# Gated linear attention: a step of 128 tokens with its state brought to the middle, and TensorE in 64x64 tiles

## The chip, the core and the metric

The kernel runs on one core of one Trainium2 chip. The metric is the time of one execution on the device, in microseconds, as the median of several runs. TensorE (PE in the profile) does matrix products and transposes, VectorE (DVE), ScalarE (ACT) and GpSimd (POOL) work on 128 partitions, SyncE (SP) issues most transfers. TensorE writes into PSUM, which has eight banks of 128 x 512 fp32. Everything here is fp32, and an fp32 product is two MATMUL records in the profile, with a weight load (PEld) before each; a transpose is one.

## The reference, cut to what matters

There are 4 batches, 8 heads, 768 tokens and 48 channels a head.

```python
f = 1.0 / (1.0 + np.exp(-f_logit))
for t in range(S):
    state = f[:, :, t, :, None] * state + np.einsum('bhd,bhe->bhde', k[:, :, t], v[:, :, t])
    y[:, :, t] = np.einsum('bhd,bhde->bhe', q[:, :, t], state)
# x = y as (4*768, 8*48)
noisy_logits = x @ w_gate + np.log1p(np.exp(x @ w_noise)) * noise
# the two best of 8 experts, softmax over the two, then
# out[token] += weight * (relu(x[token] @ w1[e]) @ w2[e])
```

Per head and channel the state decays by f and gains an outer product of k and v; y reads it with q. The 3072 rows of y then go through a router to two of eight experts, each a pair of matrices 384x1024 and 1024x384.

## The kernel before

**Attention.** It is computed in 24 steps; step n is chunk c = n // 4 of 128 tokens (C) in batch b = n % 4. Heads stand in pairs: partitions 0 to 63 hold one head of a pair and 64 to 127 the other (`rows(par)`), four pairs side by side in the free dimension (`cols(hp)`). Within a step, with L the running sum of -log f, P = exp(-L) and Q = exp(L), the kernel forms qP = q·P and kQ = k·Q. The scores sc are kQ·qP for all 128x128 pairs of tokens of a head, masked to the causal ones (A, line 575). y is A·v (line 590) plus the part that comes from the state before the step, state·qP (line 601). The state after the step is (ds + state)·P at the step's last token, with ds = kn·v (line 596) and kn the transposed kQ (lines 566 and 568).

The work on one step is spread over several turns of the loop over i at the end, so that engines rarely wait for each other. In turn i the stages are, in this order: `forget` of step i+3 (transposes of f, exp, ln), `scaled` of i+1 (transposes of q and k, products with P and Q), `scores` of i, `summed` of i+2 (the running sum), `output` of i-1 (A·v, ds, the state's part, the new state), `decays` of i+2 (P and Q), `features` of i-2 (y times the router's weights and a reordering matrix, line 625, then the sums `lg` and the copy `xs` to memory). Between stages the loop takes one piece of the router of an earlier chunk (`route`), every third time one transfer of a list entry (`puts`), and near the end the first pieces of the experts. The order in which the program is written is the order on each engine; a helper, `in_order`, fixes it.

**What sets the order around the change.** Loads of f, q, k and v are issued on SP's queue inside these stages, each into a ring (5, 4, 4 and 6 buffers) and two to four steps ahead. PSUM: one pool of six single banks, given out in turn (`one_bank`), and one pair of banks for sc (`two_banks`). y takes two of the single banks. Products of K=64 and M=128 (sc), K=128 and M=64 (A·v, ds) and K=M=64 (the state's part) use half or a quarter of TensorE's array each.

**Experts.** From the end of attention to the end of the kernel two layers per expert run from gathered rows; none of this changes, except for which bank a product gets. Half of the tokens are routed before the second half of attention, so experts start as soon as attention ends. A check that no decay left the safe range (`beyond`, line 1181) stands behind the router.

Of the kernel before, what the change touches and what calls it, by code (L numbers as in the profile page):

```python
# [331 lines left out]
def kernel(  # L332
# [57 lines left out]
    XMIN, LMAX, LCAP = -40.0, 39.0, 60.0  # L390
    assert (H * D, H * DP, B * S) == (DM, 512, N)
# [15 lines left out]
    ps1 = ctx.enter_context(tc.tile_pool(name="ps1", bufs=6, space=PSUM))  # L407
# [3 lines left out]
    turns = [ps1]  # L411

    def one_bank(name):
        turns.append(turns.pop(0))
        return turns[-1].tile([128, 512], F32, tag="one", name=name)

    def two_banks(name):
        return ps2.tile([128, 2, 512], F32, tag="two", name=name)
# [26 lines left out]
    def counting(name, pattern, base=0, by_partition=0):  # L445
# [12 lines left out]
    causal = const.tile([128, 128], F32, tag="causal", name="causal")  # L458
    nc.gpsimd.affine_select(out=causal, in_=ones, compare_op=ALU.is_ge, fill=0.0, base=0,
                            pattern=[[1, 128]], channel_multiplier=-1)  # L460
    earlier = const.tile([128, 128], F32, tag="earlier", name="earlier")
# [47 lines left out]
    logf, L, P, Q, qP, kQ, A, kn, yT, lg = ({} for _ in range(10))  # L509

    def rows(par):
        return slice(par * DP, (par + 1) * DP)

    def cols(hp):
        return slice(hp * C, (hp + 1) * C)

# [11 lines left out]
    def transposed(nm, n):  # L528
        p = one_bank(f"{nm}p_{n}")
        flat = pads[nm][n % RING[nm]].rearrange("t h d -> t (h d)")  # L530
        for hp in range(HP):
            nc.tensor.transpose(p[:, cols(hp)], flat[:, cols(hp)], ident)  # L532
        return p
# [15 lines left out]
    def decays(n):  # L549
        P[n] = wk.tile([128, HP * C], F32, tag="P", name=f"P_{n}", bufs=4)  # L550
# [3 lines left out]
        nc.scalar.copy(far[:, n, :], L[n].rearrange("d (a t) -> d a t", t=C)[:, :, C - 1])  # L554

    def scaled(n):
        qP[n] = wk.tile([128, HP * C], F32, tag="qP", name=f"qP_{n}", bufs=3)
        nc.vector.tensor_tensor(qP[n], transposed("q", n), P[n], ALU.mult)
        kQ[n] = wk.tile([128, HP * C], F32, tag="kQ", name=f"kQ_{n}")
        nc.vector.tensor_tensor(kQ[n], transposed("k", n), Q[n], ALU.mult)  # L560

    def scores(n):
        if n // B < NCH - 1:
            kp = one_bank(f"kp_{n}")
            for hp in range(HP):
                nc.tensor.transpose(kp[:, cols(hp)], kQ[n][:, cols(hp)], ident)
            kn[n] = wk.tile([C, H, DP], F32, tag="kn", name=f"kn_{n}")
            nc.scalar.copy(kn[n].rearrange("t h d -> t (h d)"), kp)
        sc = two_banks(f"sc_{n}")
        for hp in range(HP):  # L570
            for par in range(2):
                nc.tensor.matmul(sc[:, par, cols(hp)], lhsT=kQ[n][rows(par), cols(hp)],  # L572
                                 rhs=qP[n][rows(par), cols(hp)], start=True, stop=True)
        A[n] = wk.tile([C, 2, HP * C], F32, tag="A", name=f"A_{n}")
        nc.vector.tensor_tensor(A[n].rearrange("j r (a i) -> j (r a) i", i=C), sc.rearrange("j r (a i) -> j (r a) i", i=C),  # L575
                                causal.unsqueeze(1).broadcast_to((C, H, C)), ALU.mult)

    def output(n):
        c, b = n // B, n % B
        vt = pads["v"][n % RING["v"]]  # L580


        y = [one_bank(f"y{odd}_{n}") for odd in range(2)]

        def at(hp, par):
            return y[hp % 2][rows(par ^ hp % 2), cols(hp // 2)]

        for hp in range(HP):
            for par in range(2):
                nc.tensor.matmul(at(hp, par), lhsT=vt[:, 2 * hp + par, :], rhs=A[n][:, par, cols(hp)],  # L590
                                 start=(hp < 2), stop=(c == 0 and hp >= HP - 2))
        if c < NCH - 1:
            ds = one_bank(f"ds_{n}")
            for hp in range(HP):
                for par in range(2):
                    nc.tensor.matmul(ds[rows(par), hp * DP:(hp + 1) * DP], lhsT=kn[n][:, 2 * hp + par, :],  # L596
                                     rhs=vt[:, 2 * hp + par, :], start=True, stop=True)
        if c:
            for hp in range(HP):
                for par in range(2):  # L600
                    nc.tensor.matmul(at(hp, par), lhsT=state[b][rows(par), hp, :],  # L601
                                     rhs=qP[n][rows(par), cols(hp)], start=False, stop=(hp >= HP - 2))
        yT[n] = wk.tile([128, 2, HP // 2 * C], F32, tag="yT", name=f"yT_{n}")
        for odd in range(2):
            nc.scalar.copy(yT[n][:, odd, :], y[odd][:, 0:HP // 2 * C])
        if c == NCH - 1:
            return

        dsv = wk.tile([128, HP, DP], F32, tag="ds", name=f"dss_{n}")
        nc.scalar.copy(dsv, ds[:, 0:HP * DP].rearrange("d (a e) -> d a e", e=DP))  # L610
        end = P[n].rearrange("d (a t) -> d a t", t=C)[:, :, C - 1:C].broadcast_to((128, HP, DP))
        new = wk.tile([128, HP, DP], F32, tag=f"st{b}", name=f"st_{n}")
# [757 lines left out]
```

## Time and profile before

| | |
|---|---|
| median of 14 runs | 664.78 us (661.1 to 673.97) |
| the profiled execution | 664.13 us, its span 662.1 us |
| TensorE busy | 642.7 us, 97% |
| VectorE, ScalarE, GpSimd busy | 442.5, 250.1, 264.3 us |
| attention | from the start to about 150 us; sc of step 0 starts at 13.6, of step 23 at 147.4 |
| queue q1 (transfers issued by SP) | 144,912 packets, 88.7 MB |

The profile is one execution. In rows of one stretch of time, busy time of every engine stands beside its number of instructions, then the clock granted to TensorE as a share of full speed, the mean busy share of the 16 DMA engines, and GB/s. In the chain of waits each line is a start, a length and what the end of the kernel waited for in that time.

### The profile page before, as it was taken

The numbers are of one execution on the slowest core, as the hardware profiler recorded it, in microseconds if no ns is written. First come the engines' busy times: TensorE is split into PE (matmuls) and PEld (weight loads), VectorE is DVE, ScalarE is ACT, GpSimd is POOL, SyncE is SP. The second block draws the span as 40 slices with busy tenths as digits, with TensorE's granted clock in tenths as the row PEclk, the third lists the DMA queues.
The fourth block names the chain that finished last, engine by engine and source line by source line (L and its number), as shares of the span: only waits on it lengthen the run. The fifth ranks groups of instructions, "written<-read, shape, count | busy, mean of one in ns | idle before, by whom it ended". The sixth has DMA issues, their size and how long they took to land.

```text
span 662.1 us, 13307 instructions
## 1 busy us (share of the span) xinstructions
PE 642.7 (97%) x5075; PEld 586.8 (89%) x5075; DVE 442.5 (67%) x1017; ACT 250.1 (38%) x611; POOL 264.3 (40%) x300
## 2 busy tenths in 40 slices
PE   8999999998999999999999999999999999999991
PEld 8999988886999899999999898998989989889891
DVE  7777867784647455445767767776776777766751
ACT  5876757652222212222332323333233233232320
POOL 7633886863267432123404224151341523513021
PEclk9999999999999999999999999999999999999996
DMA  9999989696589865652333495572954748701112
GB/s 185 200 210 213 197 192 193 139 341 183 162 249 259 215 210 179 185 143 49 60 108 76 122 309 162 189 214 82 314 169 121 230 132 294 190 3 25 21 25 29
DMA packets 157161, 108.90 MB, mean 164 GB/s; under 512 B 115536, under 2 KB 147280, under 8 KB 157088
## 3 DMA queue, kind: packets, MB, share of 16 engines
q1 hardware_dynamic: 144912, 88.70, 48.0%
q0 software_dynamic: 12176, 19.25, 13.6%
q8 instruction: 42, 0.69, 0.5%
q14 instruction: 31, 0.25, 0.1%
HBM read 88.56 MB, written 19.62 MB: 163 GB/s over the span
## 4 chain that ended last, share of the span: by engine, by line
PE 94%; DMA 2%; issue 1%; DVE 0%; POOL 0%; SPq 0%; POOLq 0%; DVEq 0%
PE y L986 32%; PE hp L878 13%; PE P L905 7%; PE W L905 4%; PE Z L905 4%; PE V L905 4%; PE X L905 4%; PE sc L572 4%; PE xp L625 4%; PE y L590 4%; PE xgp L827 2%; PE y L601 2%; PE fp L532 2%; PE kp L532 2%; PE ds L596 1%; PE qp L532 1%
## 5 line engine op out<-in xcount | busy, mean ns | idle before, releaser
L995 POOL DMA_INDIRECT out_dram<-ys,slots x48 | 81.7, 1701 | 211.3 <-ACT ys L1052 180.1
L986 PE MATMUL y<-qk_all,f_all 128*128 128x192 f32 x576 | 105.2, 326 | 0.0
L986 PEld LDWEIGHTS y<-qk_all,f_all 128*128 128x128 f32 x576 | 93.6, 190 | 0.2 <-DVE f_all L968 0.2
L878 PE MATMUL hp<-xt,w 128*128 128x256 f32 x384 | 87.2, 382 | 1.1 <-issue 1.0
L878 PEld LDWEIGHTS hp<-xt,w 128*128 128x128 f32 x384 | 71.7, 190 | 13.4 <-issue 3.9
L986 PE MATMUL y<-w,hs 128*128 128x192 f32 x384 | 70.8, 327 | 0.0
L986 PEld LDWEIGHTS y<-w,hs 128*128 128x128 f32 x384 | 63.7, 190 | 1.2
L968 DVE TENSOR_TENSOR f_all<-hs 128x512 f32<-128x512 f32 x48 | 32.4, 690 | 41.9 <-ACT hs L880 34.2
L810 POOL DMA_INDIRECT xg<-x_rows,slots x48 | 50.8, 1059 | 18.3 <-issue 10.7
L702 POOL DMA_INDIRECT lists<-entry,sloti x48 | 51.8, 1080 | 9.8 <-issue 9.3
L880 ACT ACTIVATE hs<-hp 128x512 f32<-128x512 f32 x32 | 19.1, 597 | 68.9 <-PE hp L878 62.4
L1052 ACT ACTIVATE ys<-ys,slots 128x384 f32<-128x384 f32 x24 | 14.8, 615 | 71.2 <-DVE ys L1051 69.4
L1126 POOL DMA_INDIRECT out_dram<-ys_q,slots_q x5 | 8.6, 1716 | 80.4 <-DVE ys_q L1124 80.4
L905 PE MATMUL P<-sides,v_all 128*128 128x256 f32 x128 | 38.1, 379 | 0.0
L575 DVE TENSOR_TENSOR A<-sc,causal 128x1024 f32<-128x1024 f32 x24 | 29.3, 1222 | 11.8 <-PE sc L572 9.1
L828 ACT COPY xt<-xgp 128x384 f32<-128x384 f32 x32 | 15.3, 478 | 56.7 <-PE xgp L827 56.7
L941 ACT ACTIVATE hs<-hs 128x256 f32<-128x256 f32 x32 | 13.4, 418 | 59.4 <-DVE hs L921 56.1
L1044 DVE TENSOR_TENSOR ys<-P,y 128x192 f32<-128x192 f32 x24 | 8.5, 354 | 39.9 <-PE y L986 25.1
L986 PE MATMUL y<-qk_all,hs 128*128 128x192 f32 x192 | 35.1, 326 | 0.0
L986 PE MATMUL y<-w,f_all 128*128 128x192 f32 x192 | 35.1, 326 | 0.0
L905 PE MATMUL X<-xt,w 128*128 128x256 f32 x128 | 32.8, 379 | 0.0
L905 PE MATMUL Z<-xt,v_all 128*128 128x256 f32 x128 | 32.8, 379 | 0.0
(189 smaller groups left out, 1381.9 us busy)
## 6 DMA issues: line engine op xcount, KB each, us to landing
w<-in_moe_w_dram SPq DMA_DIRECT2D x28, 1536.0 KB
w_q<-in_moe_w_dram SPq DMA_DIRECT2D x10, 1536.0 KB
f_all<-in_f_logit_dram SPq DMA_DIRECT2D x24, 192.0 KB
qk_all<-in_q_dram SPq DMA_DIRECT2D x24, 192.0 KB
qk_all<-in_k_dram SPq DMA_DIRECT2D x24, 192.0 KB
v_all<-in_v_dram SPq DMA_DIRECT2D x24, 192.0 KB
x_rows<-xs SPq DMA_DIRECT2D x24, 192.0 KB
out_dram<-zero SPq DMA_DIRECT2D x24, 192.0 KB
```

What stands on the lines that cost most here:

```text
L532: nc.tensor.transpose(p[:, cols(hp)], flat[:, cols(hp)], ident)
L572: nc.tensor.matmul(sc[:, par, cols(hp)], lhsT=kQ[n][rows(par), cols(hp)], rhs=qP[n][rows(par), cols(hp)], start=True, stop=True)
L575: nc.vector.tensor_tensor(A[n].rearrange("j r (a i) -> j (r a) i", i=C), sc.rearrange("j r (a i) -> j (r a) i", i=C), causal.unsqueeze(1). ...
L590: nc.tensor.matmul(at(hp, par), lhsT=vt[:, 2 * hp + par, :], rhs=A[n][:, par, cols(hp)], start=(hp < 2), stop=(c == 0 and hp >= HP - 2))
L625: nc.tensor.matmul(xp[:, hp, :], lhsT=yT[n][:, hp % 2, cols(hp // 2)], rhs=w_rt[:, hp, :], start=True, stop=True)
L702: into = nc.gpsimd.indirect_dma_start(out=lists, out_offset=bass.IndirectOffsetOnAxis(ap=sloti[:, r, b:b + 1], axis=0), in_=entry[:, c, b, ...
L810: nc.gpsimd.indirect_dma_start(out=xg[p][:, s, :], out_offset=None, in_=x_rows[0:HALF * B * C] if p < E else x_rows, in_offset=bass.Indire ...
L878: nc.tensor.matmul(hp[:, o, :], lhsT=w1[home(k)][:, i, (fo + o) * 128:(fo + o + 1) * 128], rhs=xt[k][:, i, :], start=(i == 0), stop=(i == ...
L905: nc.tensor.matmul(to, lhsT=x, rhs=y, start=start, stop=stop)
L968: nc.vector.tensor_tensor(sm[which], x, y, op)
L986: nc.tensor.matmul(P[name], lhsT=x[:, o, :], rhs=y[:, o, :], start=(o == 0), stop=(o == FH - 1))
L995: into = nc.gpsimd.indirect_dma_start(out=out, out_offset=bass.IndirectOffsetOnAxis(ap=slots[p][:, s, 2:3], axis=0), in_=ys[s], in_offset= ...
```

## The change

Tokens attend to each other only within 64 of a step's 128. A state in the middle of the step, `half` = ds of the first 64 tokens + the state before, carries the rest to the second 64. So sc and A·v have two 64x64 blocks on the diagonal for each head in place of one 128x128, and ds is made apart for the two halves. The matmuls are all 64x64 tiles at 64 columns, ordered so that four that follow one another use four different quarters of the array.

- `output` is split: `advance` (ds, `half`, the new state) now belongs to the same turn as `scores`, `output` (A·v and half of the state's part) to the next, `finish` (the other half and the copy to SBUF) to the turn after that.
- `upright` (transposing kQ) is a stage of its own, a turn before, and runs in the last chunk too. `scaled` runs a turn earlier. The order of the stages in a turn is new, and loads follow it.
- PSUM: four single banks with fixed users (bank 0: q and kn, 1: k and the first ds, 2: the second ds, `features`, 3: f and the router), a pair for sc and a pair for y, each with one buffer.
- The new state is made from `half`, the second ds and P's last column, kept in `far`, which held L's.
- The clears of the output and the empty lists are issued some steps later.

```diff
-    ps1 = ctx.enter_context(tc.tile_pool(name="ps1", bufs=6, space=PSUM))
+    ps1 = ctx.enter_context(tc.tile_pool(name="ps1", bufs=1, space=PSUM))
...
+    turns = [(ps1, n) for n in (0, 1, 3)]
+
+    def one_bank(name, which=None):
+        if which is None or which != 2 and done["turned"]:
+            turns.append(turns.pop(0))
+            pool, which = turns[-1]
+        else:
+            pool = ps1
+        return pool.tile([128, 512], F32, tag=f"bank{which}", name=name)
...
     def scores(n):
-        if n // B < NCH - 1:
-            kp = one_bank(f"kp_{n}")
-            for hp in range(HP):
-                nc.tensor.transpose(kp[:, cols(hp)], kQ[n][:, cols(hp)], ident)
-            kn[n] = wk.tile([C, H, DP], F32, tag="kn", name=f"kn_{n}")
-            nc.scalar.copy(kn[n].rearrange("t h d -> t (h d)"), kp)
         sc = two_banks(f"sc_{n}")
         for hp in range(HP):
-            for par in range(2):
-                nc.tensor.matmul(sc[:, par, cols(hp)], lhsT=kQ[n][rows(par), cols(hp)],
-                                 rhs=qP[n][rows(par), cols(hp)], start=True, stop=True)
+            for par, k in ((0, 0), (1, 1), (0, 1), (1, 0)):
+                nc.tensor.matmul(sc[rows(k), par, hp * T:(hp + 1) * T], lhsT=kQ[n][rows(par), part(hp, k)],
+                                 rhs=qP[n][rows(par), part(hp, k)], start=True, stop=True)
...
+    def from_state(n, phase):
+        was, y = held[n]
+        for hp in range(0, HP, 2):
+            for par, odd in ((0, 0), (1, 0), (0, 1), (1, 1)):
+                k = par ^ phase
+                if was[k] is not None:
+                    nc.tensor.matmul(y[rows(par ^ odd), k, (hp + odd) * T:(hp + odd + 1) * T], lhsT=was[k][rows(par), hp + odd, :],
+                                     rhs=qP[n][rows(par), part(hp + odd, k)], start=False, stop=(phase == 1 and hp == HP - 2))
+
+    def finish(n):
...
+        from_state(n, 1)
+        yT[n] = wk.tile([128, HP, 2, T], F32, tag="yT", name=f"yT_{n}")
+        nc.scalar.copy(yT[n].rearrange("e a r t -> e r a t"), held[n][1][:, :, 0:HP * T].rearrange("e r (a t) -> e r a t", t=T))
+
+    def advance(n):
...
+        for hp in range(HP):
+            for k, par in ((0, 0), (1, 1), (0, 1), (1, 0)):
+                if k < len(ds):
+                    nc.tensor.matmul(ds[k][rows(par), hp * DP:(hp + 1) * DP], lhsT=kn[n][rows(k), 2 * hp + par, :],
+                                     rhs=vt[rows(k), 2 * hp + par, :], start=True, stop=True)
...
+        if c:
+            nc.vector.tensor_tensor(half, dsv[0], state[b], ALU.add)
+        else:
+            nc.vector.tensor_copy(half, dsv[0])
+        before[n] = state[b], half
+        if last:
+            return
+        dss = wk.tile([128, HP, DP], F32, tag="ds", name=f"dss_{n}", bufs=1)
+        nc.scalar.copy(dss, dsv[1])
...
+        nc.gpsimd.tensor_tensor(mid, dss, half, ALU.add)
+        nc.gpsimd.tensor_tensor(new, mid, far[:, n, :].unsqueeze(2).broadcast_to((128, HP, DP)), ALU.mult)
...
     def output(n):
...
+        y = two_banks(f"y_{n}", "y")
         for hp in range(HP):
+            for k, par in ((0, 0), (1, 1), (0, 1), (1, 0)):
+                nc.tensor.matmul(y[rows(par ^ hp % 2), k, hp * T:(hp + 1) * T], lhsT=vt[rows(k), 2 * hp + par, :],
+                                 rhs=A[n][rows(k), par, hp * T:(hp + 1) * T], start=(hp == 0),
+                                 stop=(c == 0 and k == 0 and hp == HP - 1))
+        held[n] = before[n], y
+        from_state(n, 0)
...
-    for nm, n in (("f", 0), ("f", 1), ("q", 0), ("k", 0), ("f", 2), ("f", 3), ("q", 1), ("k", 1), ("v", 0)):
+    for nm, n in (("f", 0), ("f", 1), ("q", 0), ("k", 0), ("f", 2), ("q", 1), ("k", 1), ("f", 3), ("v", 0), ("q", 2), ("k", 2)):
         load(nm, n)
...
-        for stage, lag in ((forget, -3), (scaled, -1), (scores, 0), (summed, -2), (output, 1), (decays, -2), (features, 2)):
+        for stage, lag in ((upright, -1), (summed, -2), (finish, 2), (decays, -2), (scores, 0), (advance, 0), (output, 1), (scaled, -2), (forget, -3), (features, 2)):
```

## The prediction

> **What bounds the kernel now.** I read the page's busy times first, then the stretches of the span with every engine beside the others, then the chain of waits for one step of the attention part, then ScalarE's order of time in the same step.
>
> ```profile
> span 662.1 us, 13307 instructions
> PE 642.7 (97%) x5075; PEld 586.8 (89%) x5075; DVE 442.5 (67%) x1017; ACT 250.1 (38%) x611; POOL 264.3 (40%) x300
> ```
>
> TensorE is busy for 97% of the span, so a step gets shorter only if TensorE's own list gets shorter. The shares of the other engines are averages over attention and experts; the stretch 60 to 80 us is attention alone. Its columns are the length, then busy time and instructions of TensorE, its weight loads, VectorE, ScalarE and GpSimd, then granted clock, DMA share and GB/s:
>
> ```profile
> 60.00:80.00 20.00, 20.00 (x285) 18.42 (x284) 15.76 (x46) 14.47 (x40) 13.85 (x18) 1.00 0.94 198
> ```
>
> Here VectorE stands at 79%, ScalarE at 72%, GpSimd at 69% and the DMA at 0.94. TensorE is the bound with little room behind it: a change that takes a fifth of TensorE's work brings the others to their limits. The chain of waits (start, length, what) shows one whole step between two starts of sc, 6.00 us apart:
>
> ```profile
> 32.48 1.09 PE sc L572 x16
> ...
> 66.53 0.44 PE fp L532 x4
> ...
> 67.41 0.44 PE kp L532 x4
> ...
> 68.28 1.09 PE sc L572 x16
> 69.37 1.02 PE y L590 x16
> 70.40 0.46 PE ds L596 x16
> 70.86 0.60 PE y L601 x16
> 71.46 1.08 PE xp L625 x8
> ...
> 147.36 1.09 PE sc L572 x16
> ...
> 152.86 0.97 issue
> ```
>
> Four sets of transposes at 0.44 and these five make 6.01 us, and no wait stands between them. Each matmul has two records. ScalarE in that step:
>
> ```profile
> 67.43 0.50 ACT L630 COPY xs<-xp 128x384 f32<-128x384 f32 x1
> 67.80 0.63 ACT L537 ACTIVATE f<-fp 128x512 f32<-128x512 f32 x1
> 68.46 0.63 ACT L538 ACTIVATE f<-f 128x512 f32<-128x512 f32 x1
> 69.12 0.20 ACT L541 COPY cap<-f 128x4 f32<-128x4 f32 x1
> ...
> 69.88 0.57 ACT L568 COPY kn<-kp 128x512 f32<-128x512 f32 x1
> ```
>
> The reader is to see the spacing from one start to the next: 0.37 after xs, 0.66, 0.66, 0.11 after cap.
>
> **TensorE's list.** Two spacings carry the sum. Four transposes of 128 columns take 0.44, so 0.110 each; ds, eight pairs of 64 columns, takes 0.46, so 0.058 a pair. With 0.110 for each of eight pairs sc would take 0.88, y 0.88, xp 0.88, and the state's four groups of four 0.44: what is over, 0.21, 0.14, 0.20 and 0.16, I call the entry that each change of tile shape costs. The changed step has 64x64 tiles in sc, A·v and ds: eight groups of four at 64 columns. A group of four is not in the trace at 64 columns, only at 128, in the state's rows. One cut of that stretch, for these rows alone (columns: length, TensorE busy and records, weight loads, clock, DMA):
>
> ```profile
> 76.78:76.82 0.04, 0.03 (x4) 0.03 (x4) 1.00 1.09 219
> ```
>
> Four matmuls start within 0.04 us, and the next four only 0.11 after them: four tiles do run beside each other. So a group of four at 64 columns lies between 0.058 (columns decide, as in ds) and 0.115 (two pairs, one after the other). I take 0.058, since the state's four cost no more than one transpose of as many columns. Then sc, A·v and ds cost 0.46 each, the state's two halves 0.23 each (half of them a step later, in `finish`), transposes 1.76, xp 0.88, and two entries instead of four, 0.40: 4.88 against 6.01, so 1.13 less in each of the 16 steps of chunks 1 to 4. Chunk 0 has no state's part before (5.41 a step), and after it half of the tiles but as many groups: 0.53 less. Chunk 5 has no kp and no ds before (5.11); the change keeps both there, with ds in half the tiles and as many groups: 0.23 less. Sum 16x1.13 + 4x0.53 + 4x0.23 = 21.1 us off TensorE.
>
> **What becomes late instead.** First y: the accumulator is now one tile of two banks with a single buffer, so A·v of step i-1 waits until ScalarE has copied the y of step i-2 that `finish` completed in the same step. ScalarE's order puts ahead of that copy: exp, ln and cap of f, xs, kn. From the end of fp: hand-over 0.19, 0.66, 0.66, 0.11, 0.37, kn about 0.5, the copy of 128x512 about 0.58 (kn's row; the two halves of before take 0.65), hand-over 0.1: 3.17. TensorE's list from fp's end to A·v is xp 0.88, kp 0.44, entry 0.20, finish 0.23, sc 0.46, ds 0.46: 2.67. TensorE waits 0.50. Behind it in its queue stand A·v, the half of the state's part and the next three sets of transposes; VectorE's qP and kQ wait for those. It holds in the 17 steps that still have an f to transpose: +8.5 us. Its bounds are 0 (copies ahead of it move) and 0.9 (xs late).
>
> Second the start. The stretches from 10 to 40 us move 196 to 206 GB/s at a share of 0.95 to 1.03, so a load of 196.6 KB lands each 0.98 us. The first lands at 0.81+2.65=3.46. v of step 1 is load 19 now (18 before), so it lands near 21.1. Before, y of step 1 stood behind the second step's sc at 22.8 and never felt it. Now ds belongs to step 1 itself. From 21.1: ds, A·v, half state, entry, three transposes, kp, entry, finish make 3.5, so sc of step 2 is near 24.6, of step 3 near 29.9 and of step 4 near 35.4, where it stood at 32.48: +3.0 us (bounds +1.5 and +4).
>
> Third the small ones. VectorE: A drops from 1.22 to qP's 0.69 (same shape), the new half costs between the 0.35 of a 192-column and the 0.69 of a 512-column add, I take 0.42: about 0.1 less of 4.7 a step, hidden while TensorE has 4.88. But lg now often stands behind a piece of the router (max and index, about 0.36) and xs behind it: +0.1 in 17 steps, 1.7 us (bounds 0 and 0.36 each). GpSimd: chunk 0 gains a mid of 0.75 in each of four steps and the start two small copies for the mask, chunk 5 nothing: nothing waits for the new state until four steps later. SP's queue: q and k are asked for in the same step but behind v; `finish` adds no DMA; the clears of out and the empty lists move a few steps later, behind loads that run three steps ahead. Four single-column matmuls near the end: under 0.3 each, 1 us at most, in the range.
>
> Sum against the profiled execution's 664.1: -21.1 +8.5 +3.0 +1.7 = -7.9, so 656.2. The median of the 14 runs, 664.78, stands 0.65 above it: 657.
>
> **A rule against it.** The state's rows show four starts within 0.04 us. The Trainium skill, page "TensorE: Matmul & The Clock Gate", section "Wait — 56ns, not 53.3ns?", says that starts of matmuls never come closer than about 25 ns however few columns they have. By that, 128 records of a step's tiled part would take 3.2 us in place of 1.86, the sum would end near 681, and the change would be slower. The row shows some 10 ns between starts on different tiles, so I do not use it.
>
> **Rivals.** (1) TensorE alone sets the step: ScalarE is early enough and y never waits. For it: ScalarE has 28% idle. Against: the order above. -21.1+3.0 gives 646.7. (2) The DMA sets it. 0.94 of 6.0 us is 5.64 us of transfers a step, clears included; if that is need and not queueing, 17 steps shrink by 0.37 only, with the start +3.0 : 661.5. For it: share 0.94 to 1.03. Against: loads run far ahead of use (q of step 9 is issued at 39.75 and transposed near 60.6). (3) The other side: TensorE runs out of instructions. A step has 90 matmul records before and 152 after, each with its weight load; the page's instruction queue moved 0.69 MB for TensorE's 10,150, so 12 KB a step become 21, through the same crowded engines. The 0.97 us "issue" at 152.86, which no semaphore explains, is what such a gap would look like (my reading, not shown). One such gap in each of 20 steps is +19.4, so 676.6; it decides from 0.4 us a step on. Against: at 6.0 us a step it is rare. (4) The change does not do what it says: groups of four come as two pairs, 0.115. 32 groups of 0.057 more in 24 steps is +44, less the 8.5 of waits that this hides: 692. It decides from 0.08 a group.
>
> **Numbers.** Main 0.52, (1) 0.14, (2) 0.16, (3) 0.13, (4) 0.05. Within 0.5% (3.3 us, about what this measurement can tell from no change) lie half of (2), a little of the main case and of (3). Faster 0.70, same 0.10, slower 0.20. The main case's own range, from the bounds of its three waits, is 650 to 663; with (1) and the near half of (3) 645 to 670.
>
> **What would show it.** sc and A·v at 0.46 to 0.55 for 32 records; ScalarE's yT ending just before A·v starts; a TensorE wait of half a microsecond in each step at A·v; sc of step 4 near 35 us and the last sc near 139. Wrong if ds or sc take 0.9, if unexplained gaps spread over the steps, or if waits stand at kQ or at loads.

## The result, and the profile after

The changed kernel takes 692.03 us (median of 10 runs, 689.51 to 695.16) against 665.16 us (median of 47 runs of the kernel before): a ratio of 1.040, 95% interval 1.037 to 1.043. The forecast was 657.0, range 645 to 670. It was wrong by 35 us and on the wrong side.

First the page of the changed kernel: its span, TensorE's busy time and count, and the span in 40 slices (TensorE's busy tenths, then the clock granted to it, 17.3 us a slice).

```profile
span 690.9 us, 16424 instructions
...
PE 641.2 (93%) x6635; PEld 584.2 (85%) x6635; DVE 437.9 (63%) x1041; ACT 251.0 (36%) x591; POOL 263.6 (38%) x306
...
PE   7899887775999999999999999999999999999992
...
PEclk9999999996999999999999999999999999999997
```

TensorE has 1560 more pairs of weight load and matmul than before and is busy for 641.2 us, 1.5 less than before, in a span that is 28.8 longer. The start is idle as before; the fifth to the tenth slice, 69 to 173 us, are new. The stretches say more. Columns: length, busy time and instructions of TensorE, its weight loads, VectorE, ScalarE and GpSimd, then granted clock, DMA share, GB/s.

```profile
28.00:60.00 32.00, 29.66 (x822) 27.25 (x818) 22.76 (x53) 24.85 (x63) 14.86 (x18) 1.00 0.90 191
...
80.00:100.00 20.00, 16.89 (x445) 14.91 (x445) 13.16 (x28) 12.16 (x30) 16.32 (x23) 1.00 0.87 178
...
140.00:160.00 20.00, 12.78 (x298) 11.28 (x288) 10.86 (x29) 8.76 (x21) 12.82 (x17) 0.93 1.02 340
160.00:180.00 20.00, 14.17 (x233) 12.54 (x235) 7.92 (x21) 4.46 (x12) 3.60 (x8) 0.73 0.46 118
```

From 28 to 60 us TensorE works about as forecast. From 80 to 180 us it is busy for 13 to 17 of 20 us, and no other engine takes over: VectorE falls to 8 to 13 us, ScalarE to 4 to 12. The clock is lower as well, 0.93 from 140 to 160 us and 0.73 from 160 to 180. The trace's clock rows have 20.5 us at half speed between 100 and 175 us; the kernel before has none between 9 and 650 us.

The chain of waits in a step at 35 us is the forecast's own picture (start, length, what):

```profile
35.15 0.61 ACT f L549
...
35.78 0.64 ACT f L550
...
36.44 0.20 ACT cap L553
36.64 0.38 ACT xs L661
37.02 0.49 ACT kn L579
37.50 0.50 ACT yT L609
...
38.04 0.69 PE y L646 x32
```

fp is ready, ScalarE works through exp, ln, cap, xs, kn and yT with nothing between, and A·v starts 0.04 after yT's end. A·v of neighbouring steps starts at 32.72, 38.04, 43.36 and 48.69: 5.32 apart, where the forecast's main case had 5.38. The 32 matmuls of A·v start within 0.48 us, in eight groups of four tiles, 0.058 us from group to group.

The chain in a late step is a different kernel:

```profile
153.35 0.33 PE sc L585 x18
153.69 1.03 issue
154.72 0.28 PE sc L585 x2
155.00 1.14 issue
156.14 0.29 PE sc L585 x2
...
163.53 1.14 issue
164.67 0.26 PE ds L619
```

TensorE issues one to three matmuls and then nothing for about a microsecond, over and over for twelve microseconds, and no semaphore is named. Counted from the records, weight loads included, 42 start between 153.4 and 166.0 us; each of the steps between 36 and 53 us has 272 to 310 in 5.3 to 5.4 us. Up to 175 us there are 36 such gaps of over 0.4 us from record to record without a semaphore, 23.8 us in sum; the kernel before has 8, 5.2 us in sum. Within a train the gaps follow each other every 0.70 us or twice that. What runs beside them is on GpSimd (start, length, engine, line, operation, out<-in):

```profile
155.55 0.99 POOL L733 DMA_INDIRECT lists<-entry,sloti  x1 [0.21 <-issue]
...
156.84 0.97 POOL L733 DMA_INDIRECT lists<-entry,sloti  x1 [0.23 <-issue]
...
158.11 0.97 POOL L733 DMA_INDIRECT lists<-entry,sloti  x1 [0.23 <-issue]
```

These are the indirect DMAs that write list entries (`puts`, line 733), one every 1.28 us. 34 of the 35 gaps after 65 us lie beside an indirect DMA or within a microsecond of one; so do all 8 of the kernel before, the longest of them here:

```profile
153.18 0.97 POOL L702 DMA_INDIRECT lists<-entry,sloti  x1 [0.23 <-issue]
153.83 0.27 PE L601 MATMUL y<-qP,st 64*64 64x128 f32 x1 [0.97 <-issue]
```

In both kernels 0.7 of the time from 65 to 175 us lies so near to an indirect DMA. For the 8 the match is therefore weak, for the 34 of 35 it is a pointer; the experiments decide. TensorE's waits up to 200 us (waiting line, what it waited for, sum in us, times, longest) put the rest beside them:

```profile
PE sc L585 <- issue: 8.3, 14, 1.1
PE ds L619 <- issue: 5.9, 9, 1.1
PE kp L577 <- DVE kQ L572: 4.0, 6, 1.8
PE fp L544 <- DVE at L724: 3.6, 3, 1.2
PE y L646 <- ACT yT L609: 2.0, 7, 0.3
PE kp L577 <- DVE lack L757: 1.9, 1, 1.9
```

Two of the named waits are not in the forecast: fp waits for `at` and kp for `lack`, two small readings of the router by VectorE. (Of the wait at kQ, 3.3 of the 4.0 us stand in the first 25 us.) The router's products now share bank 3 with f's transposes, or take one of the three banks that rotate, and VectorE does them behind qP and kQ.

### The profile page after: what moved, and what is told of

Its sections match the earlier page's. It is cut to its first block, busy times and chain, and to the rows that moved or that the text cites. A ratio compares the mean times of both kernels' runs of the same rounds, so it can differ in the third digit from the quotient of the medians.

```text
span 690.9 us, 16424 instructions
## 1 busy us (share of the span) xinstructions
PE 641.2 (93%) x6635; PEld 584.2 (85%) x6635; DVE 437.9 (63%) x1041; ACT 251.0 (36%) x591; POOL 263.6 (38%) x306
## 4 chain that ended last, share of the span: by engine, by line
PE 84%; issue 4%; ACT 3%; DVE 3%; DMA 2%; SPq 1%; POOL 0%; POOLq 0%; DVEq 0%; ACTq 0%
PE y L1017 31%; PE hp L909 12%; PE P L936 6%; PE Z L936 4%; PE V L936 4%; PE X L936 4%; PE W L936 4%; PE xgp L858 2%; PE y L646 2%; PE y L600 2%; PE xp L656 2%; PE sc L585 2%; PE qp L544 2%; PE ds L619 2%; DMA v_all<-in_v_dram 1%
## 5 line engine op out<-in xcount | busy, mean ns | idle before, releaser
L1026 POOL DMA_INDIRECT out_dram<-ys,slots x48 | 80.1, 1669 | 231.1 <-ACT ys L1083 195.1
L558 DVE TENSOR_TENSOR_SCAN L<-f,cap 128x512 f32<-128x512 f32 x24 | 29.9, 1244 | 9.1 <-ACT cap L553 8.2
```

The lines of the kernel that those rows point to most:

```text
L558: nc.vector.tensor_tensor_scan(L[n], data0=logf[n], data1=cap[n % 2].rearrange("d a t -> d (a t)"), initial=0.0, op0=ALU.add, op1=ALU.min)
L1026: into = nc.gpsimd.indirect_dma_start(out=out, out_offset=bass.IndirectOffsetOnAxis(ap=slots[p][:, s, 2:3], axis=0), in_=ys[s], in_offset= ...
```

## The experiments

Three theories. **B**: indirect DMAs that GpSimd issues one behind the other slow the arrival of TensorE's instructions, and the changed kernel is more sensitive. **A**, the nearest to rival (3): TensorE's instructions are fetched too late because it executes more of them. **C**: the loss is waits for VectorE, ScalarE and loads. Ratios are to the kernel before on the same chip and in the same group of runs; steps are counted by the first record of their sc. Up to e14 a step of the changed kernel is that of the profile above. When e15 ran the kernel once more, its steps 5 to 8 took 16.6 us where that profile has 17.4, so less than a microsecond between two runs says nothing.

### Without the writes, more writes, later writes

**e1.** The writes are left out.

```diff
-            into = nc.gpsimd.indirect_dma_start(
-                out=lists, out_offset=bass.IndirectOffsetOnAxis(ap=sloti[:, r, b:b + 1], axis=0),
-                in_=entry[:, c, b, r, :], in_offset=None)
```

> The changed kernel without its 48 indirect writes of list entries (the puts on GpSimd); the lists stay empty, so the gathers read row 0, the experts work on the wrong rows and nothing is added to the output: the output is not the reference's. Theory B (indirect DMAs that GpSimd issues one behind the other slow the arrival of TensorE's instructions): the 35 TensorE gaps over 0.4 us without a semaphore before 175 us (23.8 us) go down to at most 8 gaps (5 us), which lie beside the gathers of 144 to 154 us; the first hp, at 177.2 us, moves to 152 to 158; time 664 to 673. Theory A (TensorE's instruction blocks are fetched too late because it executes more instructions per microsecond): gaps and time as they are, 687 to 693. Theory C (the loss is waits for VectorE, ScalarE or loads): 687 to 693.

675.33 against 665.46 (1 run): ratio 1.015. 10 gaps with 7.4 us are left; eight of them lie at 134 to 142 us beside the six indirect reads (line 841 of the changed kernel). The first hp starts at 160.1. Each of the three lies a little beyond what theory B gave (at most 8 gaps and 5 us, 152 to 158, 664 to 673). A and C, which expected no gain, are out as main causes; but 10 us of loss are left.

**e2 and e3.** Eight further writes, into arrays that nobody reads, in steps that have none; the second in the kernel before.

```diff
+            if spares and i >= 5:
+                nc.gpsimd.indirect_dma_start(out=spares.pop(0), out_offset=bass.IndirectOffsetOnAxis(ap=line, axis=0),
+                                             in_=empty[:, 0, :], in_offset=None)
+                nc.gpsimd.memset(spacer, 0.0)
```

> The changed kernel with eight further indirect writes (128 rows of 16 bytes, each into a spare array of its own) issued by GpSimd one behind the other in the two steps from the fifth on, about 40 to 51 us, where the changed kernel has no indirect DMA and one unexplained TensorE gap. Theory B: gaps of 0.5 to 0.7 us without a semaphore appear in that stretch, 2 to 6 us in sum (0.6 us a microsecond of burst would be 6, its later steps give less beside single writes), and the time grows by as much. Theory A: none appear, since the instructions of TensorE are the same; time within 1 us. Theory C: within 1 us.

> The kernel before with the same eight further indirect writes in its fifth and sixth step. Theory B with a price per instruction: the steps of before hold 90 matmuls in 6 us against 152 in 5.3, so the gaps come to less, 0 to 2.5 us (its own bursts between 95 and 158 us have 4.5 us of gaps in 22 us). Theory B with a price per write whatever runs: as much as in the changed kernel, 2 to 6 us. Theory A: nothing.

Changed kernel: 699.74 (1.051). From step 5 to step 8 it takes 24.60 us against 17.40 without them: 7.2 us, 0.9 a write; there are 8 gaps there, 5.0 us in sum. Kernel before: 673.98 (1.013); from step 5 to 8 it takes 21.89 against 17.99: 3.9 us, 0.5 a write, with 5 gaps, 2.8 us. That is more than a price per instruction allowed (0 to 2.5) and less than the same price per write. The chain of e2 at the place of the second group of three:

```profile
50.44 0.15 PE ds L623 x2
50.58 0.42 issue
51.00 0.31 PE ds L623 x3
51.31 0.41 issue
51.72 0.63 PE ds L623 x26
```

The trains of gaps can be made at will, by adding to GpSimd's list, with TensorE's own list unchanged. This shows that the indirect DMAs hold up TensorE; that it is the arrival of its instructions that they slow, as B puts it, is not shown. A second thing is shown, by one run each: the same eight writes cost the changed kernel nearly twice as much as the one before.

**e4.** The writes of chunks 3 and 4 wait until attention is over.

```diff
-            if puts and (slot % 3 == 0 or n_routed >= HALF):
+            if puts and (slot % 3 == 0 or n_routed >= HALF) and len(n_put) < HALF * B * 2:
```

> The changed kernel with the indirect writes of chunks 3 and 4 held back until attention is over (the writes of chunks 0 to 2 stay, since the first gathers need them). Theory B: the twelve microseconds of gaps between 153 and 166 us go, and with them the low clock after it; the writes then lie beside the experts, where bursts of eight have no gap at 215 to 226 us; the gaps at 77 to 136 us stay: time 674 to 682, ratio to the kernel before 1.015 to 1.025. Theory A: 687 to 693, since the same instructions run at the same rate. Theory C: 687 to 693.

684.44, ratio 1.029 (1.022 to 1.037): the direction of B, 7.6 us less, but short of 674 to 682. The train at 153 to 166 us is gone. In its place the experts have 3.6 us of gaps beside the writes that are now there, in one row of 15 indirect DMAs from 195 to 216 us and another of 17 up to 246. In the changed kernel itself the rows beside the experts, eight at the most up to 240 us, had none.

**e11.** The same edit in the kernel before.

> The kernel before with the indirect writes of chunks 3 and 4 held back until attention is over, as in the run that did so in the changed kernel. If a burst beside the attention steps is what costs: the burst of eight at 147 to 157 us and its 2.6 us of gaps go, and the writes lie beside the experts: 1 to 4 us less, ratio 0.994 to 0.999. If the first experts' matmuls, which run from 148 us on in the kernel before, are slowed as much wherever the burst lies: 0.999 to 1.003.

670.98, ratio 1.008 (1.004 to 1.011): slower, against both expectations. The waits of TensorE from 150 us on show why:

```profile
PE hp L878 <- DVE xt L828: 4.9, 2, 4.5
```

The chain ahead of that wait, with a release that the profile cannot name:

```profile
193.48 6.19 another core or an unknown queue
...
199.76 0.35 DVE ys L1044
...
201.83 0.57 DVE xt L828
...
202.44 2.93 PE hp L878 x6
```

VectorE stands still for 6.2 us before it writes ys, and xt, which TensorE needs, stands behind it. GpSimd's list holds the indirect additions to the output that read ys, one at 184.11 and the next only at 204.73, and between them nine of the writes and two reads. That the late release of ys comes from the writes in the same queue is a reading of these rows, not shown. The burst costs in its new place too.

### What in it costs

**e5 and e6.** In the quiet steps, four other things in the place of the eight writes: e5 has writes of 16 rows (from step 5) and indirect reads (from step 8), e6 has additions on GpSimd and then plain DMAs that GpSimd issues.

```diff
+                if m < 8:
+                    nc.gpsimd.indirect_dma_start(out=spare[m], out_offset=bass.IndirectOffsetOnAxis(ap=line[0:16], axis=0),
+                                                 in_=empty[0:16, 0, :], in_offset=None)
+                else:
+                    nc.gpsimd.indirect_dma_start(out=got[m - 8], out_offset=None, in_=moe_w_gate,
+                                                 in_offset=bass.IndirectOffsetOnAxis(ap=line, axis=0))
```

```diff
+                if m < 8:
+                    nc.gpsimd.tensor_tensor(junk, junk, junk, ALU.add)
+                else:
+                    nc.gpsimd.dma_start(out=spare[m - 8], in_=empty[:, 0, :])
```

> The changed kernel with, in the quiet steps, eight indirect writes of 16 rows in place of 128 (from step 5 on, about 40 to 51 us) and then eight indirect reads of 128 rows of 32 bytes (from step 8 on, about 59 to 72 us), each one behind the other on GpSimd. If the TensorE gaps come with the descriptors that an indirect DMA brings: the writes of 16 rows, an eighth as many, give at most 0.9 us of gaps against the 5 us that the eight writes of 128 rows gave, and the reads give 3 to 6 us. If they come with each indirect DMA whatever its size: 3 to 6 us of gaps for both. If they come with writes to memory only: none at the reads. Time 695 to 705 by the first, 700 to 706 by the second.

> The changed kernel with, in the quiet steps, eight additions of 128x256 on GpSimd (from step 5 on) and then eight plain DMAs of 128 rows of 16 bytes that GpSimd issues (from step 8 on), each one behind the other. If a busy GpSimd is enough to slow the arrival of TensorE's instructions: 3 to 6 us of TensorE gaps without a semaphore beside the additions. If DMAs that GpSimd's own program prepares are what does it, indirect or not: none at the additions, 2 to 6 us at the plain DMAs. If it takes the indirect form: none at either, time within 2 us of 692.

e5: 710.68 (1.063). Steps 5 to 8 take 7.8 us more than in the changed kernel, as much as with 128 rows; steps 8 to 11 take 8.6 more. So neither the number of rows nor the direction decides. The time is above both expected ranges, which had counted the gaps alone: these come to 5.6 and 4.1 us, and beside each of the two trains the clock is at half for 6.8 us as well. e6: 693.96 (1.038, where the changed kernel itself is 1.040). Steps 5 to 8 take 0.3 more, steps 8 to 11 take 1.9 more, all of it one gap of 2.43 us at 70.94, 2.4 us after GpSimd issued the last plain DMA. The kernel's own first indirect write (71.36 to 72.51) lies within it; which of the two it belongs to, if to either, stays open. The additions cost 0.3 us here, no more than two runs differ by, and eight plain DMAs 1.9 at most. It takes the indirect form.

### The waits

**e7.** The half of the state's part and yT ahead of kp and kn, A·v ahead of ds.

```diff
-        for stage, lag in ((upright, -1), (summed, -2), (finish, 2), (decays, -2), (scores, 0), (advance, 0), (output, 1), ...
+        for stage, lag in ((finish, 2), (upright, -1), (summed, -2), (decays, -2), (scores, 0), (output, 1), (advance, 0), ...
```

> The changed kernel with two exchanges in the step's order: the second half of the state's part and the copy of y ahead of kp and kn, and A times v ahead of ds. If the wait of A times v for ScalarE's copy sets the step of 5.32 us where no indirect DMA runs: yT comes 0.6 earlier, the wait of 0.50 at A times v goes, 0.2 to 0.3 of it comes back at ds for kn; 0.2 to 0.4 less a step in some 17 steps, so the steps of 28 to 55 us are 4.9 to 5.15 apart and the time is 684 to 689. If something else holds the step (the loads, VectorE, or the instructions): steps of 5.3 and 690 to 694.

704.16, ratio 1.055 (1.049 to 1.060): slower, against the expectation. In the steps from 30 to 55 us TensorE no longer waits for anything, and yet they are 5.52 apart. One step of its chain:

```profile
36.67 0.62 PE sc L585 x32
37.29 0.67 PE y L646 x32
...
38.66 0.59 PE qp L544 x4
...
40.35 0.88 PE xp L656 x8
41.23 0.38 PE y L600 x8
41.61 0.59 PE kp L577 x4
```

The wait went, and the step became TensorE's own: it now changes the tile shape four times. kp, sc, qp and the state's half stand at 0.59, 0.62, 0.59 and 0.38, where the forecast's times without an entry are 0.44, 0.46, 0.44 and 0.23. The changed kernel's order has two such changes. The expectation had left the forecast's own entry out. But two further entries are only some 0.3 of the 0.7 us by which TensorE's own part of the step grew; k's transposes, now 0.66 instead of 0.44, and A·v, 0.67 instead of 0.47, are the rest, for a reason that was not looked into. So 4.82 of TensorE plus 0.50 of waiting was the better order. Later the waits for `at` rise from 3.6 to 5.2 us. The two, 0.2 in 17 steps and 1.6, are about half of the 9.0 us by which the profiled execution is longer; the other half is not explained.

**e8.** VectorE reads the two small products directly behind TensorE's writing them.

```diff
-        yield from pause()
         at = t([E, B], "at")
...
-        yield
         lack = rt.tile([1, E], F32, tag="lack", name="lack", bufs=1)
```

> The changed kernel with VectorE's reading of the router's two small products (at, lack) directly behind TensorE's writing them, in place of one place later in the order, where qP and kQ go ahead of it. If fp waits for at because both share a bank (1.37 us of gap at three of the chunks, and 2.1 at kp for lack): these four waits go, 3 to 5.5 us less, 686.5 to 689. If they only stood beside other waits: 691 to 693. The gaps without a semaphore stay in both.

688.01, ratio 1.032 (1.025 to 1.038), 5.7 us below 1.040. The rows of fp waiting for at and of kp waiting for lack are gone. The gaps stay, 26.6 us of them.

### No indirect DMA before the experts

**e9, e10 and e12.** The kernel before, the changed kernel, and the changed kernel with e8's edit, each without the writes and with the first six indirect reads replaced.

```diff
+            if p < 3:
+                nc.sync.dma_start(out=xg[p][:, s, :], in_=x_rows[(2 * p + s) * 128:(2 * p + s + 1) * 128, :])
+                continue
```

> The kernel before without the 48 indirect writes, and with the first six indirect reads (those of the attention part) replaced by plain reads of consecutive rows on SP's queue: the experts work on the wrong rows and the output is not the reference's. If indirect DMAs slow TensorE's instructions in the kernel before too, at half of the price per DMA that the changed kernel pays (0.5 against 1 us in the added bursts): its gaps of 5 us and some stretched steps go, 3 to 9 us less, ratio 0.986 to 0.996. If it hardly pays at all: 0.997 to 1.0.

> The changed kernel with the same two edits, so that no indirect DMA runs before the experts. If what is left of the loss without the writes (675.3, 10 us over the kernel before) is the six reads and the low clock behind them: the gaps of 134 to 141 us go (5.4 us) and some 3 to 5 us of half clock, 664 to 669, ratio 0.995 to 1.005. If it is the waits for VectorE (at, lack, kQ) and the start: 672 to 676, ratio 1.01 to 1.016.

> The changed kernel without indirect DMAs before the experts (the two edits of that run), and with at and lack read directly behind their products. If the forecast's terms for TensorE, for the wait at A times v and for the start hold, and only indirect DMAs and the shared bank were left out of it: 657 to 663, ratio 0.985 to 0.997, and not slower than the kernel before. If something else costs as much again: 668 or more.

| without indirect DMAs before the experts | time | ratio to before (interval) | gaps to 175 us |
|---|---|---|---|
| e9, kernel before | 657.81 | 0.987 (0.981 to 0.993) | none |
| e10, changed | 664.94 | 0.998 (0.995 to 1.002) | 1, 0.5 us |
| e12, changed, at and lack read at once | 658.65 | 0.988 (0.982 to 0.994) | 2, 1.9 us |

All three fell inside what was expected of the first reading. What TensorE waits for in e10 up to 200 us are semaphores, but for one gap of 0.3 us:

```profile
PE y L646 <- ACT yT L609: 4.9, 18, 0.3
PE kp L577 <- DVE kQ L572: 4.1, 6, 2.4
PE fp L544 <- DVE at L724: 3.6, 3, 1.2
PE kp L577 <- DVE lack L748: 1.9, 1, 1.9
```

The wait of A·v for yT stands 18 times at 0.27 on the average (0.50 from record to record with the hand-over). So each part has a price. The indirect DMAs cost the changed kernel 692.03 - 664.94 = 27.1 us and the kernel before 665.16 - 657.81 = 7.35: 19.7 more. The shared bank costs 664.94 - 658.65 = 6.3. What is left, 658.65 - 657.81, is 0.8. That these add up to the 26.9 which the change cost follows from how they are taken, one from the next; what the runs show is the size of each. The changed kernel itself was not run on the chip of e9 to e12, but on a second one, in e15, it took 692.17. And e8, with the indirect DMAs in place, priced the bank at 5.7. With both gone, the change is worth nothing: 0.8 us more than the kernel before without its indirect DMAs.

### Is it the closeness in time?

**e13 and e14.** The eight further writes at every third place of the order in place of every place; and the changed kernel with e8's edit and its own late writes at every third place.

```diff
-            if spares and i >= 5:
+            if spares and i >= 4 and slot % 3 == 0:
```

```diff
-            if puts and (slot % 3 == 0 or n_routed >= HALF):
+            if puts and (slot % 3 == 0 or n_routed >= HALF and len(n_put) < HALF * B * 2):
```

> The changed kernel with the same eight further indirect writes of 128 rows, but only at every third place of the order (one per 2.3 us) from step 4 on, about 36 to 56 us. If closeness in time is what costs: the steps stay 5.3 to 5.5 us apart, step 8 begins at most 2 us later than in the changed kernel (59.25), and at most two TensorE gaps over 0.4 us appear there. If each indirect DMA costs by itself: step 8 begins 5 to 8 us later, as it did with the eight in a row (66.85).

> The changed kernel, whole, with at and lack read directly behind their products, and with the indirect writes of chunks 3 and 4 at every third place of the order until attention is over. If spacing cures: the train of gaps of 12 to 15 us near 147 to 166 us shrinks to under 5 us, its 13.7 us of half clock go, and the 4 us of the shared bank go: 672 to 680, ratio 1.01 to 1.022. If each indirect DMA costs by itself: 686 to 689.

669.50 (1 run) and 669.20 (662.48 to 671.98), where the kernel before took 658.71 (657.74 to 660.27) on this chip. The profiled execution of e14, at 662.48, has eleven indirect DMAs in a row from 141 to 155 us and not one gap beside them; its other three executions took 668 to 672 at a lower clock and have no trace. Where the kernel before itself is faster and a row can pass without a gap, these two runs don't tell what was asked: the changed kernel itself had to run beside them.

**e15 to e18.** On one further chip: the changed kernel; with the eight writes in a row (e2's kernel); with the eight spaced (e13's kernel); and e14's kernel again.

> The changed kernel, unchanged, as the measure for the other three of this chip. If the cost of indirect DMAs differs from chip to chip and goes with the time of the kernel before: 690 to 697 where the kernel before takes 664 to 670; 664 to 674 where it takes 657 to 660.

> The changed kernel with the eight further indirect writes one behind the other from step 5 on. Closeness in time costs, on a chip with trains of gaps: step 8 begins 5 to 9 us later than in the changed kernel on this chip. On a chip without them: at most 2 us later, and the time within 3 us of the changed kernel's.

> The changed kernel with the same eight writes at every third place of the order from step 4 on. If closeness costs: step 8 at most 2 us later than in the changed kernel on this chip, whatever the eight in a row cost there. If each indirect DMA costs by itself: as much as the eight in a row, within 2 us.

> The changed kernel with at and lack read directly behind their products and the late writes at every third place. On a chip with trains of gaps: 8 to 18 us less than the changed kernel there if spacing cures, 3 to 6 us less (the shared bank alone) if it does not. On a chip without: 4 to 8 us less either way.

| one chip, kernel before 668.42 | time | ratio | steps 4 to 8 |
|---|---|---|---|
| e15 changed | 692.17 | 1.039 | 21.90 |
| e16 eight in a row | 703.97 | 1.057 | 31.34 |
| e17 eight spaced | 695.18 | 1.044 | 23.26 |
| e18 late writes spaced, at and lack at once | 688.00 | 1.034 | |

In a row (1.3 to 2.6 us from one to the next) the eight cost 9.4 us between steps 4 and 8; spaced (2.6 to 4.2 us, the last two 1.3) they cost 1.4. Counted as the expectations were, by the start of step 8, both are somewhat over: 9.6 us later for 5 to 9, and 2.6 for at most 2, of which 1.2 were there at step 4 already. The stretches 44 to 52 and 52 to 60 us (same columns as above), first of e16, then of e17:

```profile
44.00:52.00 8.00, 6.10 (x133) 5.10 (x129) 3.35 (x7) 5.24 (x15) 7.12 (x13) 0.96 0.79 160
52.00:60.00 8.00, 6.35 (x84) 5.22 (x78) 2.70 (x8) 0.86 (x3) 6.10 (x10) 0.50 0.79 174
```

```profile
44.00:52.00 8.00, 7.26 (x250) 6.64 (x241) 5.91 (x12) 6.68 (x17) 7.41 (x9) 1.00 0.87 182
52.00:60.00 8.00, 7.32 (x167) 6.34 (x166) 5.96 (x20) 5.04 (x13) 7.05 (x12) 1.00 0.77 154
```

GpSimd is busy for about as long in both. In a row, TensorE starts 84 matmuls in the second stretch and the clock falls to 0.50; spaced, 167 and 1.00. It is the closeness in time that costs. The same kernels also show how far chips differ: e13's takes 669.50 on the one and 695.18 on the other, e14's 669.20 and 688.00.

e18 gained 4.2 us, within the 3 to 6 that were expected from the bank alone; its late train (13.0 us of gaps from 146 to 162) stayed. GpSimd's rows say why:

```profile
152.56 0.99 POOL L732 DMA_INDIRECT lists<-entry,sloti  x1 [0.22 <-issue]
...
153.86 0.97 POOL L732 DMA_INDIRECT lists<-entry,sloti  x1 [0.22 <-issue]
```

The writes were spaced in the program's order, but in the last chunk GpSimd has no state to compute between them, waits for nothing, and issues them 1.28 us apart as before. A place in the order holds an engine back only where something stands there.

## Why the prediction was wrong, point by point

- **Groups of four at 0.058 us, two entries, TensorE's step of 4.88:** right. A·v 0.47 and the state's half 0.23, and 5.32 less the wait of 0.50 is 4.82. Rival (4) is out; that its 692 is the time measured is chance. The rule weighed there, of the Trainium skill (page "TensorE: Matmul & The Clock Gate", section "Wait — 56ns, not 53.3ns?": no two starts closer than about 25 ns), does not agree with this trace: 64 records (32 matmuls, 32 weight loads) start within 0.48 us, 7.5 ns apart, on different tiles.
- **A·v waits 0.50 for yT, 17 times:** right in place, size and number: 0.5 from record to record, 18 times in e10, 8.8 us in sum. Rival (1) is out with it.
- **Rival (2), the DMA sets the step at 5.64:** out; steps of 5.32.
- **The start, +3.0:** 3.9 between e9 and e12 (sc of step 4 at 32.64 and 36.53), inside +1.5 to +4. The chain has the 5.17 us of v's load that the forecast named, ds of step 1 starting at 21.82. It did not name the waits at kQ, 3.3 us in these first steps, which were one of its signs of being wrong.
- **The sum:** two errors of arithmetic and size. The +3.0 was read at step 4, after chunk 0, and so already held chunk 0's 4x0.53 = 2.1, which the 21.1 then counted again. And VectorE's router pieces were put at 1.7. From step 8 to 20, e12's steps take 5.73 where the quiet ones take 5.35 (e10, steps 4 to 8): 4.6 us over twelve steps, of which the waits at kQ are 0.9. In e9 the same steps grow too, from 6.00 to 6.11, so some 3.3 us belong to the change; they were not taken apart. The end, from sc of step 20 to the last instruction, came out 3.1 longer than in e9 (529.2 and 526.1) where 0.4 shorter was forecast. Of this, 0.9 stands between the sc of steps 20 and 22 (11.29 and 10.35 us); the rest was not taken apart. The change's own terms, measured by e12 against e9, come to +0.8 and not to -7.9.
- **The bank, never priced:** the forecast listed "PSUM: four single banks with fixed users" and looked only at y's single buffer for a wait. f and the router share bank 3, and fp waits behind `at`, and kp behind `lack`: 3.6 + 1.9 us of waits, 6.3 us of time.
- **The step that failed: rival (3).** "One such gap in each of 20 steps is +19.4 ... Against: at 6.0 us a step it is rare." The symptom was named, a gap without a semaphore that the trace calls issue, and with it the sign "if unexplained gaps spread over the steps". It is what made the time: 27.1 us of the changed kernel's, 7.35 of the kernel's before, so 19.7 of the 26.9 that the change cost. But the sum had no term for it, and the rival tied it to the number of instructions and to the crowded instruction queue, from a single gap at 152.86, and was put at 0.13. What the runs showed in its place is that GpSimd's indirect DMAs, which the change leaves as they are, hold up TensorE's issue, and hold up the new list more. The kernel before has 8 of these gaps, and all 8 stand beside indirect DMAs or within a microsecond of one; listing them would have pointed at a partner to try out. A price to start from was there too: 38 indirect DMAs stand before 175 us in both kernels, and 5.2 us of gaps are 0.14 each. It comes to 0.19 each in the kernel before by e9, and to 0.71 in the changed one by e10. (16 later ones are left out there too, but the last 420 us are equally long in all four kernels.)
- **Is it late fetching of instructions (A)?** For one kind of gap it may be: 13 of 16 profiled executions with the changed attention have a gap of 0.5 to 1.7 us at one and the same place of TensorE's list, its 2241st record (weight loads and waiting records counted). In the changed kernel that is at 55.14 us, with no indirect DMA near and 0.10 us after the end of a block of 16 KB that the instruction queue moved (54.16 to 55.04). Since the gap begins when the block is there, what it waits for stays open. The Trainium skill, page "Runtime: NRT & Kernel Launch", section "Instruction fetch mechanics", says that instructions come in such blocks of 256, fetched ahead, and that the cost of crossing from one to the next is mostly hidden; a gap at this one place of the quiet steps and none at their other blocks agrees with that. The trains are another matter: between the block that ends at 157.86 and the next, which starts at 173.55, TensorE starts over 300 records. If this queue brings TensorE's instructions (54 blocks of 256 for its 13,270 records), they were there while it issued a few every 0.7 us.
- **Why the changed kernel pays more per write** (0.9 against 0.5 in e2 and e3, 27.1 against 7.35 in all) is argued, not shown: it has 272 to 310 records in a step of 5.3 us where the kernel before has some 160 to 167 in that time between 36 and 55 us, and the same pause holds up more of them. The clock, at half for 20.5 us (6.8 us in e10, none in the kernel before), is a second cost on top: 10 us at the very most, less in fact, since 8.9 of the 20.5 us lie within the late train.

## What to carry to other kernels

List every gap that no semaphore explains, in the kernel before, and look at what runs on the other engines in that microsecond; what cost 7 us in the kernel before cost 27 in the changed one, whose steps have 152 smaller matmuls in place of 88. Eight indirect DMAs in a row cost the changed kernel 0.9 to 1.2 us each here, with 16 rows as with 128, written or read, and 0.2 when all but the last two stood 2.6 us or more apart; spacing must come from work on the issuing engine, not from its place in the program. Where buffers become fixed banks, price each pair of users that now share one, the small ones of a side job too.

## What the hardware showed that was not expected

- Indirect DMAs that GpSimd issues one behind the other hold up TensorE's issue: gaps of 0.5 to 0.7 us, most of them with one to ten records between, and 0.9 to 1.2 us of time a DMA in the changed kernel, with 16 rows as with 128, reading as well as writing; eight additions on GpSimd cost 0.3 us in all. The Trainium skill, page "SBUF — State Buffer", section "SBUF: two separate sides", says that the ports of engines and of DMAs are apart, so that neither can slow the other. These runs don't speak of ports, but an engine was slowed beside DMAs; by what path stays open.
- It differs from chip to chip: the kernel before took 658.7 us on one chip of the experiments and 665 to 669 on the four others, the same changed kernels 669.5 and 669.2 on that one and 695.2 and 688.0 on another, and on that one an execution of e14 had eleven such DMAs in a row without a gap. Why is not known.
- Beside the experts, whose matmuls have 192 or 256 columns, rows of eight to twelve had no such gaps in either kernel; in e4 rows of 15 and 17 had 3.6 us of them, in e11 a row of 17 had none (TensorE stood waiting for xt beside its end).
